# One PSUM tile and one exponential for four heads' scores, ScalarE statistics for one tile of the first norm, a q map with a minimum, and an attention sum on GpSimd

## The chip, the core and the metric

The kernel runs on one core of a Trainium2 chip. A core has a matrix engine (TensorE, PE in the profile, with its weight loads shown apart as PEld), a vector engine (VectorE, DVE), a scalar engine for functions of one argument (ScalarE, ACT), a general engine (GpSimd, POOL), and an engine that here only issues DMAs (SyncE, SP). Each engine works through its own list of instructions in order and waits on semaphores for the others. PSUM is the memory that matmuls write; SBUF holds everything else. The metric is device time in microseconds (us) of one execution; the median of several runs counts.

## What is computed

The input is x, 2048 tokens by 512, in bf16. A layer A (attention) and a layer B (a gated feed-forward network) follow one another twice, with the same weights in both rounds:

```python
x = x + A(layernorm(x)); x = x + B(layernorm(x))     # twice

# A: H = 32 heads of 16, N = 4 segments of L = 512 tokens
phi = lambda t: where(t > 0, t + 1, exp(t))
for s in range(N):
    logits = einsum('bhqd,bhkd->bhqk', qs, ks) * scale + mask      # causal
    a_dot = softmax(logits) @ vs
    a_mem = (phi(qs) @ M) / (phi(qs) @ z + 1e-6)
    outs.append(g * a_mem + (1 - g) * a_dot)                       # g = sigmoid(beta), one per head
    M = M + phi(ks)^T @ vs;  z = z + sum(phi(ks))
A = concat(outs) @ wo

# B: F = 1792
B = (gelu(x @ w_gate) * (x @ w_up)) @ w_down
```

## The kernel before

**Stages.** Two rounds of four segments are eight stages, k = 0 to 7, of 512 tokens each. Each stage has its norm, its products for q, k and v, its scores and their use, the output product wo, and its feed-forward part (gate, up, down). Large products are written as four matmuls on column tiles of 32 (`product`, L514 to L519).

**Who sets the order.** The instructions of all engines are put in order when the program is built, by a planner written in the kernel itself. It keeps a clock for each engine (`Clocks`), adds a fixed cost for each piece of work, and knows when each result should be there. Work for TensorE lies in `items`, sorted by due times (tables `DUE` and `BIAS`); an item is opened when its inputs are ready and one of the M_BANKS = 4 PSUM banks of kind m is free. Work for the other engines is posted with `post`, with a slack by which it may stand back. What comes out is a fixed list for each engine; on the chip only semaphores hold it together. When nothing is ready while scores remain, the planner inserts a warm product, which computes nothing that is used.

**Scores.** Each stage has STEPS = 20 score steps; a step is for four heads. `score_now` decides whether the next step is due, and whether both halves of it (two heads each) or only one: both if both PSUM score tiles are free by the planner's clock, one alone if TensorE is idle or in the stages below HALF_STEPS = 2. The list `st_free` holds when each half's tile is free. `scores` (L950 to L1008) writes the score matmuls (L971) into the tiles st0 and st1, one for each half and each of two banks, then for each half one exponential on ScalarE from PSUM to SBUF (L1002, 128 x 1024, pt<-st in the profile) and the causal masks on GpSimd (L989). Both tiles have a single buffer:

```python
            sts = {n: psp.tile([P, 2, L], F32, tag=f"st{n}", bufs=1, name="st") for n in halves}
```

Scores of even heads read k from the tile kf, those of odd heads from its copy kB.

**Use of the scores.** `flush_item` (L1010 to L1117) multiplies the probabilities with the values (pt and vaug, L1036), whose extra column per head holds a constant so that the row sum comes with the product. Then DVE transposes (L1060), takes the reciprocal (L1064), scales into ab (L1068), transposes back into aT (L1075) and adds the memory's part, aT + amT (L1079). A flush is ready when all masks of its steps are done by the planner's clock.

**Around them.** The class Norm (L529 to L628) takes the statistics of four token tiles (`stats` L543, `aggr` L552), on POOL their variance plus epsilon (L560) and its power -0.5 (rs, L566), and writes the normed rows xn (L580): on DVE, but on POOL in stage k = 5, which XNP = 32 says. `phi_q` (L755 to L773) makes phi of q from an exponential (L761), a clamp (L764) and an add with two inputs (L768). `upd` and `mem` (L802 to L926) carry M and z; mblk (L899) is a 32 x 128 piece on POOL. The very first norm (L1269 to L1320) is written out by hand, since nothing runs beside it: `first_stats` (L1276) and `first_aggr` (L1279) on DVE for four tiles, `first_scale` (L1282 and L1284) on POOL for two tiles at a time. `gate` (L459) prepares sigmoid(beta) on DVE, and L456 copies the constant column into three value tiles (vaugs) on ScalarE.

## Time and profile before

| | |
|---|---|
| runs | 549.41, 549.94, 551.12 us |
| median | 549.94 us |
| profiled execution | 549.15 us |
| its span | 547.2 us |
| mean granted TensorE clock | 1.0 |
| masks on POOL (L989) | 416, of 128 x 256 (336), 128 x 512 (72) and 128 x 1024 (8) |
| attention adds on DVE (L1079) | 28: 20 of 128 x 512, mean 541 ns, and 8 of 128 x 256, mean 281 ns |
| xn on POOL (L580) | 4, mean 2088 ns |
| DMA traffic | 28.90 MB in all, mean 53 GB/s |

The profile is of one execution, taken on the chip. The span runs from the first to the last instruction; the execution's own time has 2 us more. The profiled execution lies 0.8 us below the median, so a sum that starts from its rows starts from 549.15 and has to be moved by 0.8 us to be compared with medians. A line "L1002" is line 1002 of the kernel before; "pt<-st" are the names of what is written and read. In a group's row, "x320 | 309.6, 1029 | 53.7 <-PE st L971 47.9" says 320 instructions, 309.6 us busy, 1029 ns each on average, 53.7 us idle just before them, of which 47.9 ended with a score matmul. In a timeline, the two numbers in front are the start and the length in us of a run of like instructions, which overlap in TensorE's pipeline, so the distance between starts is what a step costs there.

### The profile page before, as it was taken

Reading aid. Unit: us, or ns where it says so; the run is one execution under the profiler, and the core shown is the slowest. Engines: PE = TensorE matmul, PEld = TensorE weight load, DVE = VectorE, ACT = ScalarE, POOL = GpSimd, SP = SyncE. Lnnn points to the kernel's source line nnn. Section 1 sums busy time; section 2 is a strip of 40 time slices with the busy share of each in tenths; the row PEclk is TensorE's granted clock in tenths of the full one; section 3 lists DMA queues with packets and bytes.
Section 4 is the critical chain, followed back from the end, with each engine's and each line's share of the span. In section 5 each row is a group of like instructions: output and inputs, shape, how many; then the busy total and the mean of one; then the engine's idle time right before and its main releaser. Section 6 shows DMA issues by size and latency. Waiting matters only on the chain.

```text
span 547.2 us, 25413 instructions
## 1 busy us (share of the span) xinstructions
PE 541.5 (99%) x11388; PEld 267.9 (49%) x11388; DVE 431.4 (79%) x814; ACT 443.3 (81%) x533; POOL 259.3 (47%) x516
## 2 busy tenths in 40 slices
PE   8999999999999999999999999999999999999997
PEld 4333345344454444444444444444445445445997
DVE  5988996899869989679776898589876999777162
ACT  5999999998999778977799879997889777882600
POOL 4786674556624678147551465056643472121000
PEclk9999999999999999999999999999999999999999
DMA  7357710622123025301140123111530113102101
GB/s 232 49 151 192 139 37 6 158 30 50 32 50 62 3 41 80 51 13 22 22 70 2 23 41 60 32 17 27 80 60 4 22 22 75 27 2 52 32 5 41
DMA packets 69756, 28.90 MB, mean 53 GB/s; under 512 B 59216, under 2 KB 69200, under 8 KB 69648
## 3 DMA queue, kind: packets, MB, share of 16 engines
q1 hardware_dynamic: 69504, 27.28, 25.0%
q8 instruction: 89, 1.46, 1.2%
q14 instruction: 19, 0.16, 0.1%
q10 hardware_dynamic: 144, 0.01, 0.0%
HBM read 9.71 MB, written 2.10 MB: 22 GB/s over the span
## 4 chain that ended last, share of the span: by engine, by line
PE 95%; POOL 2%; DVE 1%; DMA 1%; ACT 1%; issue 0%; POOLq 0%
PE m L519 76%; PE st L971 11%; PE m L1036 7%; POOL xn L580 2%; PE m L884 1%; DMA x_sb<-in_A_x_dram 1%; ACT pt L1002 1%; DVE st L1276 0%; POOL pt L989 0%; PE m L623 0%; DVE st L543 0%; PE m L936 0%; DVE x_sb L1134 0%; PE m L931 0%; POOL rs L566 0%
## 5 line engine op out<-in xcount | busy, mean ns | idle before, releaser
L1002 ACT ACTIVATE pt<-st 128x1024 bf16<-128x1024 f32 x320 | 309.6, 1029 | 53.7 <-PE st L971 47.9
L989 POOL TENSOR_SCALAR_AFFINE_SELECT pt<-pt 128x512 bf16<-128x512 bf16 (+2 forms) x416 | 204.5, 510 | 221.4 <-ACT pt L1002 213.7
L519 PE MATMUL m<-xnT,wu_sb 128*32 128x512 bf16 (+1 forms) x2016 | 106.6, 356 | 0.0
L519 PE MATMUL m<-xnT,wg_sb 128*32 128x512 bf16 (+1 forms) x2016 | 106.4, 356 | 0.0
L519 PE MATMUL m<-wd_sb,gel 128*32 128x512 bf16 (+2 forms) x1848 | 106.5, 373 | 0.0
L1223 DVE TENSOR_TENSOR gel<-gel,m 128x512 bf16<-128x512 bf16 x112 | 75.2, 683 | 36.0 <-PE m L519 30.0
L519 PEld LDWEIGHTS <-wu_sb 128*32 128x32 bf16 x2016 | 51.6, 97 | 40.0 <-issue 6.1
L519 PEld LDWEIGHTS <-wg_sb 128*32 128x32 bf16 x2016 | 51.6, 97 | 38.1 <-issue 4.4
L519 PEld LDWEIGHTS <-gel 128*32 128x32 bf16 x1848 | 50.8, 97 | 39.5 <-issue 5.0
L1060 DVE STREAM_TRANSPOSE byq<-m 128x512 f32<-128x512 f32 x64 | 45.4, 710 | 21.4 <-PE m L1036 21.0
L1134 DVE TENSOR_TENSOR x_sb<-x_sb,m 128x512 bf16<-128x512 bf16 (+1 forms) x65 | 42.2, 665 | 14.8 <-PE m L519 14.7
L1036 PE MATMUL m<-pt,vaug 128*32 128x256 bf16 (+3 forms) x1088 | 46.9, 293 | 0.5 <-POOL pt L989 0.4
L971 PE MATMUL st<-q,kB 32*128 32x256 bf16 (+3 forms) x544 | 40.9, 291 | 0.0
L543 DVE BATCH_NORM_STATS2 st<-x_sb 128x6 f32<-128x512 bf16 x60 | 40.5, 676 | 0.4
L971 PE MATMUL st<-q,kf 16*128 16x256 bf16 (+3 forms) x544 | 39.8, 294 | 0.1
L1036 PEld LDWEIGHTS <-vaug 128*32 128x32 bf16 x1088 | 25.2, 97 | 22.1 <-issue 5.9
L519 PE MATMUL m<-xnT,wq_sb 128*32 128x512 bf16 x496 | 34.2, 381 | 0.0
L519 PE MATMUL m<-xnT,wk_sb 128*32 128x512 bf16 x496 | 33.9, 380 | 0.0
L1188 ACT ACTIVATE gel<-m 128x512 bf16<-128x512 f32 x56 | 30.7, 602 | 3.6 <-PE m L519 3.4
L519 PE MATMUL m<-wv_sb,xnT 128*32 128x512 bf16 x512 | 33.5, 380 | 0.0
L971 PEld LDWEIGHTS <-kf 16*128 16x128 bf16 x544 | 12.4, 91 | 43.0 <-issue 41.7
L519 PE MATMUL m<-wo_sb,aT 128*32 128x512 bf16 x512 | 31.6, 380 | 0.0
(95 smaller groups left out, 550.7 us busy)
## 6 DMA issues: line engine op xcount, KB each, us to landing
out_dram<-x_sb SPq DMA_DIRECT2D x15, 128.0 KB, 1.8
wg_sb<-in_B_w_gate_dram SPq DMA_DIRECT2D x8, 224.0 KB, 3.6
kB<-kf SPq DMA_DIRECT2D x28, 64.0 KB, 2.9
wu_sb<-in_B_w_up_dram SPq DMA_DIRECT2D x8, 224.0 KB, 3.8
wd_sb<-in_B_w_down_dram SPq DMA_DIRECT2D x7, 256.0 KB, 3.9
x_sb<-in_A_x_dram SPq DMA_DIRECT2D x3, 512.0 KB, 6.5
xnT<-xn SPq DMA_TRANSPOSE x56, 2.5
x_sb<-in_A_x_dram SPq DMA_DIRECT2D x4, 128.0 KB, 3.0
```

What stands on the lines that cost most here:

```text
L519: nc.tensor.matmul(out[r], lhsT=lhsT[:, r], rhs=rhs, start=start, stop=stop, tile_position=(0, 32 * c))
L543: nc.vector.bn_stats(out=self.st6[:, 0, :], in_=x_sb[:, self.tt0 + j, :])
L580: eng.tensor_scalar(out=xn[:], in0=x_sb[:, self.tt0 + j, :], scalar1=self.mv[:, j, 0:1], scalar2=self.rs[:, j, :], op0=ALU.subtract, op1=A ...
L884: nc.tensor.matmul(psm()[r, b, :], lhsT=self.phik[:, j, b * P + 32 * c:b * P + 32 * c + 32], rhs=by_head(self.vaug)[:, j, h:h + 2, 0:DH], ...
L971: nc.tensor.matmul(sts[j // 2][:, j % 2, c0:c0 + q1 - q0], lhsT=lhsT[rows, b, P * ki:P * ki + P], rhs=self.q[rows, b, q0:q1], start=True, ...
L989: nc.gpsimd.affine_select(out=dv, in_=dv, pattern=[[0, w], [1, P]], compare_op=ALU.is_ge, fill=0.0, base=0, channel_multiplier=-1)
L1002: 1.024, lambda st=st, tile2=tile2: nc.scalar.activation(out=tile2[:], in_=st[:], func=ACT.Exp, scale=SCALE), told), table="exp")
L1036: nc.tensor.matmul(ps()[32 * j:32 * j + 32, q0 + shift:q1 + shift], lhsT=self.vaug[:, ki, h * (DH + 1):h * (DH + 1) + 32], rhs=step["pt"][ ...
L1060: nc.vector.transpose(out=self.byq[:, c], in_=ps()[:])
L1134: ck.dve.post(ck.made(), slack, (0.15 + 0.533 * n / D, lambda: nc.vector.tensor_tensor(out=xt, in0=xt, in1=ps()[:, 0:n], op=ALU.add), lamb ...
L1188: return lambda: nc.scalar.activation(out=out(), in_=in_(), func=ACT.Gelu_apprx_tanh)
L1223: ck.dve.post(ck.made(), NORMAL, (0.683, lambda: nc.vector.tensor_tensor(out=hidden(g, h), in0=hidden(g, h), in1=banked(ps), op=ALU.mult), ...
```

## The change

In words, in the order of the diff:

- The two score tiles become one, st, of 128 x 4 x 512 in PSUM (four banks, one buffer), and so do the two tiles for probabilities.
- From k = 1 on (JOIN = 1) a step that is scored whole has one exponential, 128 x 2048, instead of two of 128 x 1024, and its masks cover four heads instead of two. Where a step is scored in halves, there are still two exponentials, on two parts of the tiles. In k = 0 there are always two.
- In the first norm ScalarE takes the sum and the sum of squares of the fourth tile with two accumulating activations, and DVE scales them; the constant column of two value tiles goes to POOL, and the gate's two small operations are posted for later.
- phi of q becomes min(exp(q), max(q, 0) + 1): one operation with two scalars and one with two inputs, instead of a clamp and a three-way add.
- aT + amT is written for GpSimd instead of VectorE.
- xn is always on VectorE.
- The planner's constants and tables (N3, FLUSH_WAIT, LAST_FIRST, SHIFT, HALVED, DUE, BIAS and others) have other values, so the order on all engines is another. The tables are left out below.

```diff
 M_BANKS = 4
+JOIN = 1
...
-N3 = 0.0
+N3 = 44.0
...
-FLUSH_WAIT = 5.228
+FLUSH_WAIT = -0.017
...
-XNP = 32
...
-LAST_FIRST = 8
+LAST_FIRST = 2
...
+HALVED = {NK - 1}
+SHIFT = 0.8
...
+    st = psp.tile([P, 4, L], F32, tag="st", bufs=1, name="st")
...
-        nc.scalar.activation(out=by_head(va)[:, :, :, DH], in_=cden[:].unsqueeze(1).to_broadcast([P, TPS, H]),
-                             func=ACT.Copy)
+    def sums_column(i):
+        return by_head(vaugs[i])[:, :, :, DH], cden[:].unsqueeze(1).to_broadcast([P, TPS, H])
...
+        ck.dve.post(14.0, NORMAL, (0.6, gate, None))
...
-            if self.on_pool:
-                ck.pool.post(ready, self.slack, (1.62, xn, told))
-            else:
-                ck.dve.post(ready, self.slack, (0.5, xn, told))
+            ck.dve.post(ready, self.slack, (0.5, xn, told))
...
-            def clamp():
-                nc.vector.tensor_scalar(out=self.phiq[:, two, :], in0=self.phiq[:, two, :], scalar1=1.0, scalar2=None,
-                                        op0=ALU.min)
-
-            def add():
-                nc.vector.scalar_tensor_tensor(out=self.phiq[:, two, :], in0=self.q[:, two, :], scalar=0.0,
-                                               in1=self.phiq[:, two, :], op0=ALU.max, op1=ALU.add)
+            def linear():
+                self.lin = wrk.tile([P, 2, L], BF16, tag="lin", bufs=1, name="lin")
+                nc.vector.tensor_scalar(out=self.lin[:], in0=self.q[:, two, :], scalar1=0.0, scalar2=1.0,
+                                        op0=ALU.max, op1=ALU.add)
+
+            def least():
+                nc.vector.tensor_tensor(out=self.phiq[:, two, :], in0=self.phiq[:, two, :], in1=self.lin[:], op=ALU.min)
 
             ck.act.post(max(ready, ck.pe), slack, (1.06, exp, lambda t: ck.dve.post(
-                t, PHI_SLACK, (0.47, clamp, None),
-                (1.29, add, lambda t2: ev.update({("phiq", self.k, b): t2 for b in (2 * half, 2 * half + 1)})))), table="exp")
+                t, PHI_SLACK, (0.47, linear, None),
+                (0.75, least, lambda t2: ev.update({("phiq", self.k, b): t2 for b in (2 * half, 2 * half + 1)})))), table="exp")
...
-                pt = [wrk.tile([P, 2, L], BF16, tag="pt", bufs=2 * PT_STEPS, name="pt") for _ in range(2)]
+                pt = wrk.tile([P, 4, L], BF16, tag="pt", bufs=PT_STEPS, name="pt")
...
-            sts = {n: psp.tile([P, 2, L], F32, tag=f"st{n}", bufs=1, name="st") for n in halves}
...
-                    nc.tensor.matmul(sts[j // 2][:, j % 2, c0:c0 + q1 - q0], lhsT=lhsT[rows, b, P * ki:P * ki + P],
+                    nc.tensor.matmul(st[:, j, c0:c0 + q1 - q0], lhsT=lhsT[rows, b, P * ki:P * ki + P],
...
-            for n in halves:
-                st, tile2 = sts[n], pt[n]
-                blocks = tile2[:].rearrange("p j (a c) -> p j a c", c=P)
-                flat = tile2[:].rearrange("p j (a c) -> p (j a) c", c=P)
-                where = {(0, 1, 2, 3): [(flat, 8)], (0, 2): [(flat[:, 0:8:2, :], 4)]}.get(
-                    diag, [(blocks[:, :, a, :], 2) for a in diag])
+            joined = halves == (0, 1) and k >= JOIN
+            for n0, n1 in [(0, 2)] if joined else [(n, n + 1) for n in halves]:
+                heads, w = slice(2 * n0, 2 * n1), 2 * (n1 - n0)
+                blocks = pt[:, heads, :].rearrange("p j (a c) -> p j a c", c=P)
+                flat = pt[:, heads, :].rearrange("p j (a c) -> p (j a) c", c=P)
+                where = {(0, 1, 2, 3): [(flat, 4 * w)], (0, 2): [(flat[:, 0:4 * w:2, :], 2 * w)]}.get(
+                    diag, [(blocks[:, :, a, :], w) for a in diag])
                 done = []
-                step["masked"].append(done)
-                st_free[n] = 1e9
+                step["masked"].append((n1 - n0, done))
+                st_free[n0:n1] = [1e9] * (n1 - n0)
 
                 def mask(dv, w):
                     nc.gpsimd.affine_select(out=dv, in_=dv, pattern=[[0, w], [1, P]], compare_op=ALU.is_ge,
                                             fill=0.0, base=0, channel_multiplier=-1)
 
-                def told(a, n=n, where=where, done=done):
-                    st_free[n] = a
+                def told(a, n0=n0, n1=n1, where=where, done=done):
+                    st_free[n0:n1] = [a] * (n1 - n0)
                     if not where:
                         done.append(a)
                         return
...
                                               for m, (dv, w) in enumerate(where)])
 
                 ck.act.post(max(begun + 0.4, step["at"]), EXP_SLACK, (
-                    1.024, lambda st=st, tile2=tile2: nc.scalar.activation(
-                        out=tile2[:], in_=st[:], func=ACT.Exp, scale=SCALE), told), table="exp")
+                    0.17 + 0.427 * w, lambda heads=heads: nc.scalar.activation(
+                        out=pt[:, heads, :], in_=st[:, heads, :], func=ACT.Exp, scale=SCALE), told), table="exp")
...
-                    nc.vector.tensor_tensor(out=self.aT[:, b, where], in0=self.aT[:, b, where],
+                    nc.gpsimd.tensor_tensor(out=self.aT[:, b, where], in0=self.aT[:, b, where],
...
-                        ck.when(lambda: ("amT", k, b) in ev, lambda: ck.dve.post(
-                            max(t, ck.pe), soon, (0.18 + 0.0167 * nq, add, there)))
+                        ck.when(lambda: ("amT", k, b) in ev, lambda: ck.pool.post(
+                            max(t, ck.pe), soon, (0.2 + 0.08 * nq, add, there)))
...
+    sums = wrk.tile([P, 1, 2], F32, tag="sums", bufs=1, name="sums")
+    junk = wrk.tile([P, L], BF16, tag="e0", bufs=1, name="junk")
+    nc.scalar.activation(out=junk[:], in_=x_sb[:, TPS - 1, :], func=ACT.Copy, scale=-1.0 / D, accum_out=sums[:, :, 0])
+    nc.scalar.activation(out=junk[:], in_=x_sb[:, TPS - 1, :], func=ACT.Square, bias=sums[:, 0, 0:1], accum_out=sums[:, :, 1])
+    nc.scalar.activation(out=sums_column(0)[0], in_=sums_column(0)[1], func=ACT.Copy)
...
-    first_stats(3)
-    first_aggr(3)
+    nc.vector.tensor_tensor(out=n0.mv[:, TPS - 1:TPS, :], in0=sums[:], in1=parts[:], op=ALU.mult)
...
-    a0.made()
-    n0.first_rows = [n0.normed(j, j) for j in range(2)]
-    gate()
-    n0.first_rows += [n0.normed(j, j) for j in range(2, TPS)]
+    a0.made[0](), a0.made[1]()
+    n0.first_rows = [n0.normed(j, j) for j in range(TPS)]
```

## The prediction

> **What bounds the kernel now.** I read the page's busy shares first, then its chain, then the timelines of TensorE (PE) and ScalarE (ACT) in the first segment, where the change rearranges most.

> ```profile
> PE 541.5 (99%) x11388; PEld 267.9 (49%) x11388; DVE 431.4 (79%) x814; ACT 443.3 (81%) x533; POOL 259.3 (47%) x516
> ...
> PE 95%; POOL 2%; DVE 1%; DMA 1%; ACT 1%; issue 0%; POOLq 0%
> ...
> L1002 ACT ACTIVATE pt<-st 128x1024 bf16<-128x1024 f32 x320 | 309.6, 1029 | 53.7 <-PE st L971 47.9
> ```

> TensorE is busy for 541.5 of 547.2 us and carries 95% of the chain; the other three engines have at least a fifth of the span to spare. Removing work from ACT, DVE or Pool therefore earns nothing by itself. What counts is TensorE's own instructions, and any gap put between them. The next windows (start:end, length, then busy us of PE, PEld, DVE, ACT and POOL, clock, DMA share, GB/s) show how little gap there is now:

> ```profile
> 12.00:110.00 98.00, 97.90 (x1856) 40.91 (x1856) 84.03 (x163) 95.38 (x117) 61.94 (x127) 1.00 0.48 106
> 110.00:300.00 190.00, 189.51 (x3896) 87.63 (x3892) 157.39 (x298) 166.89 (x201) 102.60 (x202) 1.00 0.22 38
> ```

> In the first 98 us TensorE lacks 0.1 us, at full clock, and ACT is almost as full (95.4 of 98). That is where an exponential and the score after it can least afford to wait for each other. Today they do not: the two halves of a step (two heads each) have PSUM tiles of their own, so PE scores one half while ACT reads the other.

> ```profile
> 30.55 9.60 ACT L1002 ACTIVATE pt<-st 128x1024 bf16<-128x1024 f32 x10
> ...
> 34.05 0.39 PE L971 MATMUL st<-q,kf 16*128 16x512 bf16 x2
> 34.37 0.40 PE L519 MATMUL m<-xnT,wk_sb 128*32 128x512 bf16 x4
> 34.70 0.39 PE L971 MATMUL st<-q,kf 16*128 16x512 bf16 x2
> 35.02 0.62 PE L519 MATMUL m<-xnT,wk_sb 128*32 128x512 bf16 x8
> 35.46 0.39 PE L519 MATMUL m<-xnT,wq_sb 128*32 128x512 bf16 x4
> 35.78 0.39 PE L971 MATMUL st<-q,kf 16*128 16x384 bf16 x4
> 36.10 0.73 PE L1036 MATMUL m<-pt,vaug 128*32 128x512 bf16 x16
> 36.77 0.39 PE L971 MATMUL st<-q,kf 16*128 16x384 bf16 x4
> ```

> Ten exponentials run back to back at 0.96 us each. From score to score TensorE needs 0.65 us with one product between (34.05 to 34.70), 1.08 with three (34.70 to 35.78), so 0.86 with two, and 0.99 with a flush (35.78 to 36.77). Nothing waits.

> **Part 1: one PSUM tile for four heads.** This is the term that decides. The new tile st serves all steps, also those whose halves are still scored apart: 9 steps of k=0 and 10 of k=1 in the order that the changed program, built, issues. There the first matmul of a step's second half carries a semaphore count that is reached only by the exponential of the *same* step's first half, though that reads the other two heads; and the first half waits for the previous step's second exponential. Before, each half waited for its own half of the step before. So a pair that overlapped becomes a round: score, exponential, score. Its length comes from these rows:

> ```profile
> 11.67 0.40 PE L971 MATMUL st<-q,kf 16*128 16x512 bf16 x4
> ...
> 12.10 1.94 ACT L1002 ACTIVATE pt<-st 128x1024 bf16<-128x1024 f32 x2 [1.89 <-PE st L971]
> ...
> 43.34 2.85 ACT L1002 ACTIVATE pt<-st 128x1024 bf16<-128x1024 f32 x3 [0.52 <-POOL pt L989]
> ...
> 44.41 0.39 PE L971 MATMUL st<-q,kf 16*128 16x512 bf16 x2
> ```

> From a score's start to its exponential's start 0.43 us (11.67 to 12.10); the exponential 1.02 (1029 ns on the page; 43.34 to 44.36 for the first of three here); from its end to the score that it frees 0.05 (44.36 to 44.41). Together 1.50 us for each half. TensorE takes its instructions in order, so whatever is queued behind the waiting score (products, flushes) waits too; the products that lie between two scores cover only their own 0.65 to 1.08 us. In the built order 38 such edges lie in or behind split steps: 17 with two products, 6 with a flush, 6 with three products, one each at 0.65, 0.77 and 1.04 (mixtures, by the same rows), 6 long enough to wait for nothing. The stall is 17 x 0.64 + 6 x 0.51 + 6 x 0.42 + 0.85 + 0.73 + 0.46 = 18.5 us. Five more edges lead from a step scored whole to a split one, where 0.05 + 0.43 + 1.94 = 2.42 is needed and 1.49, 1.71, 1.82, 2.04 and 2.36 are there: 2.7. In the one long row of single exponentials (k=1) two evictions by ACT of some 0.6 us stand between: about 0.7 of them is seen. Together **+21.9**; if a half takes 1.40 to 1.60 us, 18 to 26.

> From k=1 on, the steps scored whole have one exponential of 128x2048. It isn't in the trace; between 1.88 (1029 ns and twice the 427 by which it exceeds ScalarE's gelu of half its width, 602 ns at L1188) and 2.06 (twice 1029) I take 1.9, by the 1.94 of a pair in a row. It removes 130 instructions and some 20 us of ACT work, all beside TensorE: nothing. The first half's probabilities come later by 0.9 us, which I count under part 3.

> **Part 2: the order on TensorE.** 19 steps are split instead of 23. A half takes PE as long as a whole (0.32 us to the next instruction at 34.05, and 0.32 at 35.78), and the product between two scores takes 0.33 where 0.22 is its usual distance (two in 0.44 at 35.02): 0.42 for each split, -1.7. Two more warm products at 0.22: +0.4. Everything else on TensorE has the same count and shape.

> **Part 3: off TensorE.** The four xn that GpSimd (POOL) computed in one norm go to DVE. They took 8.30 us, masks stood behind them, and TensorE's starts fall 0.94 us behind there, of which its row names 0.42:

> ```profile
> 203.13 8.30 POOL L580 TENSOR_SCALAR xn<-x_sb,mv,rs 128x512 bf16<-128x512 bf16 x4
> 211.40 2.71 POOL L989 TENSOR_SCALAR_AFFINE_SELECT pt<-pt 128x256 bf16<-128x256 bf16 x6
> 211.86 0.64 PE L1036 MATMUL m<-pt,vaug 128*32 128x384 bf16 x6 [0.42 <-POOL pt L989]
> ```

> That goes: -0.9. The 28 attention adds go from DVE (0.54 us each) to POOL. POOL's nearest row with the same shape is xn at 2.09; by the growth of its masks with width (0.456, 0.697, 1.116 us for 256, 512 and 1024 columns) it would be lower, so I take 1.4, between 0.54 and 2.09: 39 us against 37 saved on masks (416 become 250: 72 x 0.456 + 144 x 0.697 + 30 x 1.116 + 4 x 2.0 = 175 instead of 212) and 8 on xn. POOL stays at half busy. What it can cost: a mask queued behind an add, and so a flush. From score to last mask takes about 3.1 us now with 2.3 to spare before the flush; with the joined exponential it is 3.4, and the built order puts most flushes 3.4 to 4.2 us behind their score. That cover is thin: +0.8, from 0 to 5. The q map as a minimum saves DVE some 7 us of its 1.30 us adds, beside TensorE: nothing. At the start ACT takes the fourth tile's statistics off DVE, but the reciprocal root behind it stays on POOL: -0.2 (-0.6 to +0.2).

> **Sum**: 21.9 - 1.7 + 0.4 - 0.9 - 0.2 + 0.8 = +20.3 us. The profiled execution took 549.15 us (span 547.2), so 569.5 on its scale; the median of the runs, 549.94, lies 0.8 above it, so **570.2 us**. A difference of about 0.3% (1.65 us) is what a measurement of this kernel can tell from none.

> **Rivals.** *Not slower* (0.05): the score's wait ends before it binds, because a half's round is no longer than the work between two scores. It decides at 0.86 us a round, the commonest distance. Then only the small terms are left, -1.6: 548.3, on the border of faster and same. For it: no exponential holds up a score anywhere in the trace of before. Against it: the 1.02 us exponential alone, wholly inside the round, is already longer than 0.86.

> *The clock falls* (0.08): with a wait after every half, TensorE is busy in little over half of these stretches. At the start of before, where it had just begun, its warm products stood 0.427 us apart until about 5 us, and 0.21 after. At that pace the work between the scores of the 32 stalled edges, 17 x 0.86 + 6 x 0.99 + 6 x 1.08 + 2.5 = 29.5 us, would take 59 instead of 29.5 + 18.5: +11, so 581. Against it: no wait here is longer than 1 us, and by the page the clock stays at full from its second slice to the end.
> [...]

> *POOL's adds hold up flushes* (0.07): from k=2 on slack is 0.1 to 0.7 us, and an add ahead of a flush's last mask delays it by up to 1.4. If 8 of the 28 do so by 1 us, +8: 578. For it: masks of 256 columns beside DVE's scaling of ab took 0.77 us on average where 0.41 is their median, so POOL and DVE hold each other up. Against it: POOL is idle half of the time.
> [...]

> **How the numbers follow.** Serial halves as summed: 0.80, own range 562 to 578 (a round of 1.40 to 1.60, flush waits of 0 to 5). The range has to hold 8 in 10: nine tenths of that case (0.72), the POOL case (0.07) and part of the clock case, so 561 to 581. Faster 0.03 and same 0.03 are the not-slower case with a little for a smaller stall; slower is the rest, 0.94.

> **What would show it.** In the changed kernel's profile: waits of "PE st" for "ACT pt" of about 0.5 to 0.65 us each, some 30 of them, all before k=2; single exponentials about 1.5 us apart from start to start in k=1; TensorE some 20 us short of full in the first 130 us, at clock 1.0; the joined exponential near 1.9 us; no xn on POOL. Later windows as full as before. If TensorE is gap-free in the first 130 us, the prediction is wrong at its main step; if it is full there and short later, POOL's adds are the cause; if the clock is under 1.0, the second rival.

## The result, and the profile after

The changed kernel took 576.53 us (median; 575.11 to 577.78), the kernel before 550.36 us beside it: ratio 1.0475, interval 1.0446 to 1.0504, or 26.2 us slower. The forecast was 570.2 us in a range of 561 to 581. The profiled execution took 576.83 us, its span 575.0.

First the page of the changed kernel: busy times, the granted TensorE clock in 40 slices, the chain that ended last, and the group of the exponentials.

```profile
PE 558.2 (97%) x11396; PEld 268.1 (47%) x11396; DVE 419.5 (73%) x793; ACT 438.0 (76%) x402; POOL 239.2 (42%) x378
...
PEclk9979965799999999999999999999999999999999
...
PE 89%; ACT 8%; issue 1%; DMA 1%; SPq 0%; DVE 0%; ACTq 0%
...
L1029 ACT ACTIVATE pt<-st 128x2048 bf16<-128x2048 f32 (+1 forms) x190 | 304.4, 1609 | 84.2 <-PE st L997 66.3
```

ScalarE has come onto the chain with 8%, and the clock row, all nines before, has a hole in its third slice (29 to 43 us) and a longer one from the sixth to the eighth (72 to 115 us). TensorE is busy 16.7 us longer with eight matmuls more, which is the mark of a slower clock, and idle 11.1 us longer (16.8 of its span instead of 5.7): together the 27.8 us of the span. The same two windows as before show where:

```profile
12.00:110.00 98.00, 86.18 (x1204) 31.41 (x1199) 61.52 (x126) 70.18 (x80) 49.70 (x106) 0.79 0.35 79
110.00:300.00 190.00, 189.71 (x4040) 89.47 (x4036) 154.78 (x294) 165.13 (x143) 91.72 (x129) 1.00 0.27 46
```

In the first 98 us TensorE lacks 11.8 us, its clock is 0.79 on average, and it gets through 1204 instructions instead of 1856. After 110 us it is as full as it was. The list of TensorE's waits, empty of scores before, is headed by this (us in total, times, longest):

```profile
PE st L997 <- ACT pt L1029: 10.9, 22, 0.9
```

The chain in order of time shows the round itself (start, length, what), first at full clock, then at half clock:

```profile
32.83 0.41 PE st L997 x4
33.24 0.02 issue
33.26 1.03 ACT pt L1029
34.29 0.04 issue
34.33 0.40 PE st L997 x2
...
82.48 0.62 PE st L997 x4
83.10 0.02 issue
83.12 1.03 ACT pt L1029
84.15 0.04 issue
84.19 0.62 PE st L997 x2
```

Score, exponential, score, with nothing in parallel: 1.50 us from 32.83 to 34.33, as worked out in the prediction, and 1.71 from 82.48 to 84.19, where the score takes 0.62 instead of 0.41.

### The profile page after: what moved, and what is told of

It is laid out like the page before. It is cut to its first block, busy times and chain, and to the rows that moved or that the text cites. A ratio compares the mean times of both kernels' runs of the same rounds, so it can differ in the third digit from the quotient of the medians.

```text
span 575.0 us, 25060 instructions
## 1 busy us (share of the span) xinstructions
PE 558.2 (97%) x11396; PEld 268.1 (47%) x11396; DVE 419.5 (73%) x793; ACT 438.0 (76%) x402; POOL 239.2 (42%) x378
## 4 chain that ended last, share of the span: by engine, by line
PE 89%; ACT 8%; issue 1%; DMA 1%; SPq 0%; DVE 0%; ACTq 0%
PE m L542 70%; PE st L997 11%; ACT pt L1029 7%; PE m L1063 6%; DMA x_sb<-in_A_x_dram 1%; PE m L911 0%; SPq L389 0%; PE m L641 0%; ACT kf L534 0%; PE m L963 0%; PE m L958 0%; ACT junk L1317 0%; ACT junk L1316 0%; ACT vaug L534 0%; ACT e L811 0%
## 5 line engine op out<-in xcount | busy, mean ns | idle before, releaser
L1029 ACT ACTIVATE pt<-st 128x2048 bf16<-128x2048 f32 (+1 forms) x190 | 304.4, 1609 | 84.2 <-PE st L997 66.3
L1016 POOL TENSOR_SCALAR_AFFINE_SELECT pt<-pt 128x512 bf16<-128x512 bf16 (+3 forms) x250 | 166.1, 678 | 248.2 <-ACT pt L1029 247.1
L542 PEld LDWEIGHTS <-gel 128*32 128x32 bf16 x1848 | 46.2, 97 | 44.6 <-issue 4.2
L1063 PE MATMUL m<-pt,vaug 128*32 128x256 bf16 (+3 forms) x1088 | 48.5, 303 | 0.0
L997 PEld LDWEIGHTS <-kf 16*128 16x128 bf16 x544 | 14.1, 92 | 53.2 <-issue 52.4
L1063 PEld LDWEIGHTS <-vaug 128*32 128x32 bf16 x1088 | 27.3, 99 | 22.8 <-issue 5.2
L542 PE MATMUL m<-xnT,wq_sb 128*32 128x512 bf16 x496 | 36.3, 396 | 0.0
L542 PE MATMUL m<-wo_sb,aT 128*32 128x512 bf16 x512 | 36.3, 410 | 0.0
L1106 POOL TENSOR_TENSOR aT<-aT,amT 128x512 bf16<-128x512 bf16 (+1 forms) x28 | 28.3, 1018 | 19.1 <-DVE aT L1102 14.9
L542 PE MATMUL m<-xnT,wk_sb 128*32 128x512 bf16 x496 | 36.1, 400 | 0.0
```

The lines of the kernel that those rows point to most:

```text
L542: nc.tensor.matmul(out[r], lhsT=lhsT[:, r], rhs=rhs, start=start, stop=stop, tile_position=(0, 32 * c))
L997: nc.tensor.matmul(st[:, j, c0:c0 + q1 - q0], lhsT=lhsT[rows, b, P * ki:P * ki + P], rhs=self.q[rows, b, q0:q1], start=True, stop=True, ti ...
L1016: nc.gpsimd.affine_select(out=dv, in_=dv, pattern=[[0, w], [1, P]], compare_op=ALU.is_ge, fill=0.0, base=0, channel_multiplier=-1)
L1029: 0.17 + 0.427 * w, lambda heads=heads: nc.scalar.activation(out=pt[:, heads, :], in_=st[:, heads, :], func=ACT.Exp, scale=SCALE), told), ...
L1063: nc.tensor.matmul(ps()[32 * j:32 * j + 32, q0 + shift:q1 + shift], lhsT=self.vaug[:, ki, h * (DH + 1):h * (DH + 1) + 32], rhs=step["pt"][ ...
L1106: nc.gpsimd.tensor_tensor(out=self.aT[:, b, where], in0=self.aT[:, b, where], in1=self.amT[b][:, where], op=ALU.add)
```

## The experiments

All times are medians, with the kernel before in the same series.

**Two tiles again.** The changed kernel, with the PSUM tile split; nothing else in the order of TensorE, VectorE and SyncE differs.

```diff
-    st = psp.tile([P, 4, L], F32, tag="st", bufs=1, name="st")
+    sts = [psp.tile([P, 2, L], F32, tag=f"st{n}", bufs=1, name="st") for n in range(2)]
...
-                    nc.tensor.matmul(st[:, j, c0:c0 + q1 - q0], ...
+                    nc.tensor.matmul(sts[j // 2][:, j % 2, c0:c0 + q1 - q0], ...
...
-                        out=pt[:, heads, :], in_=st[:, heads, :], func=ACT.Exp, scale=SCALE), told)
+                        out=pt[:, 2 * n:2 * n + 2, :], in_=sts[n][:], func=ACT.Exp, scale=SCALE)
+                        for n in range(n0, n1)], told)
```

> The changed kernel with the score tile split again into two PSUM tiles of two heads each; every joined exponential becomes two of 128x1024 (about 20 us more ScalarE work), all else and the order on TensorE, VectorE and SyncE unchanged. Theory (the one tile makes a half wait for the other half's exponential): the waits of scores for exponentials go, the clock stays at 1.0, and what is left are the small terms, 548.5 us (547 to 550.5). Rival (the new order, the adds on GpSimd or the longer latency cost most of it): 560 us or more, with TensorE short of full after 110 us too.

Measured: 549.14 us against 550.45, ratio 0.9976 (0.9955 to 0.9998), clock 1.0. Its two windows:

```profile
12.00:110.00 98.00, 97.30 (x1856) 40.92 (x1852) 83.36 (x164) 94.82 (x118) 59.92 (x118) 1.00 0.43 102
110.00:300.00 190.00, 189.95 (x3916) 88.34 (x3908) 156.97 (x297) 168.29 (x202) 90.16 (x127) 1.00 0.24 40
```

The 11.8 us that TensorE lacked are 0.7, and no score waits for an exponential. The rival, that the order or the adds on POOL cost most of it, falls: the whole loss (26.2 us, and the 1.3 that come free) hangs on the shared tile. This run also takes the joined exponential apart; the one called Mixed, below, keeps it from k = 2 on and is as fast, so there the joining is not the cause.

**One tile in the kernel before.** The other direction: only this part of the change.

```diff
+    st4 = psp.tile([P, 4, L], F32, tag="st", bufs=1, name="st")
...
-            sts = {n: psp.tile([P, 2, L], F32, tag=f"st{n}", bufs=1, name="st") for n in halves}
...
-                st, tile2 = sts[n], pt[n]
+                st, tile2 = st4[:, 2 * n:2 * n + 2, :], pt[n]
```

> The kernel before with one change, the two score tiles made one tile of four heads; two exponentials as before, order unchanged. Theory: the same serial rounds, in 23 split steps instead of 19 and with some whole steps following within 2.4 us, so about 25 to 30 us of waits, and some 6 us more where the clock falls: 580 us (570 to 590), clock below 1.0 in the first 110 us. Rival (the tile alone is harmless, the loss comes from the order that was made with it): 553 us or less.

Measured: 584.16 us, ratio 1.061 (1.0567 to 1.0652), or 33.7 us slower; clock of the profiled run 0.968. First its list of waits, then ScalarE's timeline where the kernel before had ten exponentials in 9.60 us:

```profile
PE st L972 <- ACT pt L1003: 17.9, 36, 1.2
...
29.88 1.02 ACT L1003 ACTIVATE pt<-st 128x1024 bf16<-128x1024 f32 x1 [0.78 <-PE st L972]
31.65 1.02 ACT L1003 ACTIVATE pt<-st 128x1024 bf16<-128x1024 f32 x1 [0.75 <-PE st L972]
33.43 1.02 ACT L1003 ACTIVATE pt<-st 128x1024 bf16<-128x1024 f32 x1 [0.76 <-PE st L972]
```

They start 1.77 us apart there, at half clock (0.73 on average from 30 to 45 us). The tile alone does it, and does more than in the changed kernel, whose order has fewer split steps: of its 17.9 us of waits 6.6 come after 110 us, where the changed kernel has 0.2, and its clock falls four times instead of three (0.968 on average over the span, against 0.964). How much of the difference each of these makes is not shown.

**Filling the waits.** To part the clock from the waits, the changed kernel computes during them: up to two products after each split half are issued twice.

```diff
+        if fills[0]:
+            fills[0] -= 1
+            product_once(out, lhsT, rhs, start, False)
+            start = False
+        product_once(out, lhsT, rhs, start, stop)
...
         att[k].scores(t, halves)
+        fills[0] = 2 if k < 2 and halves != (0, 1) else 0
```

> The changed kernel with up to two products after each score half of k=0 and k=1 issued twice, 65 in all, 14 us of TensorE work at full clock, so that it computes while it would wait; those products count twice in their sums. Theory (the clock is granted by how full TensorE is, and its fall costs about 6 us on top of the waits): the clock stays at 1.0 and the time falls though work was added, to about 570.5 us (568 to 573). Rival (the fall has another cause, or costs nothing because the waits only get shorter): clock near 0.96 again and 576 us or more.

Measured: 571.98 us, ratio 1.0394 (1.0354 to 1.0434): 21.5 us over the kernel before instead of 26.2, though TensorE does 14 us more (65 products; four matmuls take 0.216 us in the changed kernel at full clock, the median distance of their starts). From its page:

```profile
PE 555.8 (98%) x11656; PEld 277.3 (49%) x11656; DVE 419.3 (74%) x793; ACT 438.4 (77%) x402; POOL 239.3 (42%) x378
...
PEclk9999999999999999999999999999999999999999
```

The clock stays full, 1.0 on average. So the waits by themselves are worth at most 571.98 less 549.14, 22.8 us (an added product that finds no wait would add its own time), and the clock's fall at least 4.6 on top (the two intervals leave about 2.7 either way). The rounds say that the added products cost next to nothing: ahead of the first fall, six single exponentials in a row take 7.67 us from the first start to the last in both kernels (25.59 to 33.26 in the changed one, 26.07 to 33.74 here). And they give the same price for the clock: the three longest rows of single exponentials last, from first start to last, 14.55, 4.79 and 29.83 us in the changed kernel and 13.77, 4.59 and 26.03 here, 4.8 us less.

**No split steps.**

```diff
-        return (0,) if free[0] and (idle and k >= HALF_FROM or k < HALF_STEPS and not other) else ()
+        return ()
```

> The changed kernel without split steps: every step is scored whole, and the order is made anew, so it allows for the wait. Theory: a whole step frees the tile 2.42 us after its start (k=0) or 2.36 (joined), which the order knows and fills with products; ScalarE is nearly full in the first 98 us, so a part is lost there: 555 us (550 to 562), clock 1.0, few waits of scores for exponentials. Rival (the loss is ScalarE's rate behind one buffer, not the order's ignorance): 570 us or more.

Measured: 566.72 us, ratio 1.0291 (1.0253 to 1.033). This missed its range of 550 to 562, and lies below the 570 of its rival. The order allows for the wait, but finds too little to put there. First the warm products' group in this kernel, then in the changed kernel, then this kernel's windows:

```profile
L542 PE MATMUL m<-warm 128*32 128x512 bf16 x308 | 23.2, 409 | 1.0 <-DVE am L866 0.5
```

```profile
L542 PE MATMUL m<-warm 128*32 128x512 bf16 x56 | 4.3, 384 | 0.0
```

```profile
12.00:110.00 98.00, 94.64 (x1952) 43.84 (x1952) 79.55 (x160) 89.51 (x105) 52.79 (x97) 1.00 0.48 113
110.00:300.00 190.00, 185.34 (x3748) 84.01 (x3744) 151.09 (x277) 152.71 (x117) 90.38 (x129) 0.98 0.18 32
```

There are 77 warm products instead of 14 (four matmuls each), the 63 more some 13.6 us of computing for nothing at 0.216 each, and TensorE lacks 3.4 and 4.7 us in the two windows: 2.5 us are four scores that wait for an exponential, the rest are other waits. The clock falls here too, once, for the 6.8 us behind a stretch from 148.52 to 151.93 us in which TensorE was busy for 1.39 of 3.41 us. ScalarE does less than before in the same time (89.5 of 98 us instead of 95.4). That with one buffer it stands still during each score is an estimate, from the 0.48 us that single exponentials of the changed kernel waited for theirs at full clock (33.26, 34.76); that this, and not the planner's skill, sets the 566.7 us is not shown.

**Mixed.** Two tiles while steps are split (k below 2), one tile and the joined exponential after.

```diff
+            if k == 2 and t == 0:
+                one_tile()        # closes the pool of the two tiles and opens one of 128 x 4 x 512
...
-                    nc.tensor.matmul(sts[j // 2][:, j % 2, c0:c0 + q1 - q0], ...
+                    nc.tensor.matmul((whole[0][:, j] if whole else sts[j // 2][:, j % 2])[:, c0:c0 + q1 - q0], ...
```

> The changed kernel with two score tiles in k=0 and k=1, where steps are split, and the one tile with joined exponentials (128x2048) from k=2 on, where every step is whole; k=1's whole steps have two exponentials; order on TensorE, VectorE and SyncE as in the changed kernel. Theory (only split steps pay for the one tile, and the joined exponential is off the path): the same as with two tiles throughout, 549 us (547.5 to 550.5), clock 1.0, ScalarE some 17 us less busy than there. Rival (joined exponentials bring their masks, and so the flushes, too late): 551 us or more, with waits of pt matmuls for masks after k=2.

Measured: 548.62 us against 549.87, ratio 0.9973 (0.9949 to 0.9997), clock 1.0: the same as two tiles throughout, within the intervals. The masks are in time: the only wait of a pt matmul for one in its list is of 0.3 us, in k = 0. But ScalarE is only 7 us less busy (434.8 instead of 442.0), not 17. Its two forms:

```profile
L1041 ACT ACTIVATE pt<-st 128x2048 bf16<-128x2048 f32 x120 | 225.4, 1878 | 56.1 <-PE st L1009 41.6 <-POOL pt L1028 13.0 <-POOL mblk L934 0.9
L1043 ACT ACTIVATE pt<-st 128x1024 bf16<-128x1024 f32 x80 | 76.3, 1031 | 4.7 <-PE st L1009 4.5
```

A joined exponential takes 1.88 us; two in a row took 1.94, since their ends overlap (80 take 76.3, not 82.5). Joining saves 0.06 us a step, 7 in all.

**The sums on VectorE.** Two tiles throughout, with the other engine for aT + amT.

```diff
-                    nc.gpsimd.tensor_tensor(out=self.aT[:, b, where], in0=self.aT[:, b, where],
+                    nc.vector.tensor_tensor(out=self.aT[:, b, where], in0=self.aT[:, b, where],
```

> The kernel with two tiles throughout, and the 28 attention sums written for VectorE again at the places where the order has them for GpSimd. Theory (the sums are off the path on either engine): within 1 us of the kernel with two tiles, 549 us (548 to 550.5). Rival (on GpSimd they block VectorE's two-input operations and cost several us): 546 us or less.

Measured: 549.59 us against 549.87, ratio 0.9988 (0.9969 to 1.0007). With the sums on GpSimd it was 0.9976 and 0.9973. Either engine will do; the rival falls.

**Fullness and clock.** A kernel of its own, whose stages hold TensorE at different shares of its time. A line of STAGES reads products per round, exponentials per round, rounds.

```python
STAGES = [(None, 0, 120), (4, 1, 27), (None, 0, 60), (3, 1, 27), (None, 0, 60), (2, 1, 27), (None, 0, 60), (1, 1, 27),
          (None, 0, 60), (6, 2, 17), (None, 0, 60), (4, 2, 17), (None, 0, 60)]
```

> A kernel that computes none of the reference: it copies x to the output, and beside that TensorE runs stages of about 40 us. In four of them a round is a score (two matmuls), one exponential of 128x1024 that reads it, and 4, 3, 2 or 1 products of the kernel's form, so that TensorE computes for about 1.3, 1.1, 0.86 or 0.65 of 1.50 us; in two, two exponentials and 6 or 4 products, about 1.7 or 1.3 of 2.46 us. Between them it runs 60 products without a pause. Theory (the clock goes by how full TensorE is over some us, and pauses of 0.2 to 0.85 us are enough): 1.0 with 4 products, under 1.0 after a few us with 2 and 1, 3 products in between and open; of the two longer rounds 4 products falls too. Rival (only an idle stretch of some us closes the gate): 1.0 in every stage.

This is one execution. At full clock rounds came out at 1.56 us and, with two exponentials, at 2.62. The first fence has the windows of the stages with 4 and 3 products, then, in steps of 5 us, the beginning of the stage with 2, and a score there with the wait ahead of it; the second the stage with 6 products and two exponentials, a score there, and the beginning of the last stage, with 4.

```profile
32.00:70.00 38.00, 33.33 (x444) 12.48 (x436) 0.00 (x0) 25.06 (x25) 0.00 (x0) 1.00 0.00 1
87.00:125.00 38.00, 27.86 (x344) 9.86 (x337) 0.00 (x0) 24.77 (x25) 0.00 (x0) 1.00 0.01 2
...
140.00:145.00 5.00, 3.12 (x38) 0.90 (x30) 0.00 (x0) 3.38 (x4) 0.00 (x0) 1.00 0.00 0
145.00:150.00 5.00, 3.98 (x30) 0.99 (x30) 0.00 (x0) 2.80 (x4) 0.00 (x0) 0.58 0.02 3
...
141.03 0.39 PE L59 MATMUL st<-wide,w 16*128 16x512 bf16 x2 [0.63 <-ACT pt L67]
```

```profile
267.00:300.00 33.00, 22.36 (x326) 9.02 (x326) 0.00 (x0) 25.61 (x26) 0.00 (x0) 1.00 0.00 1
...
273.26 0.39 PE L59 MATMUL st<-wide,w 16*128 16x512 bf16 x2 [0.82 <-ACT pt L67]
...
320.00:325.00 5.00, 2.50 (x40) 0.91 (x32) 0.00 (x0) 3.92 (x4) 0.00 (x0) 1.00 0.00 0
325.00:330.00 5.00, 3.38 (x34) 0.97 (x31) 0.00 (x0) 4.09 (x4) 0.00 (x0) 0.67 0.00 0
```

Busy for 88% (33.33 of 38) and 73% (27.86 of 38), the clock stays at 1.0. At 62% (3.12 of 5) it is half within 10 us, and with one product too (0.50 from 212 to 245 us). In the longer rounds 68% (22.36 of 33) stays at 1.0 and 50% (2.50 of 5) falls, to 0.67 in the next 5 us. In these stages the share decides, not the length of one pause: at 68% TensorE stood still for 0.82 us of each 2.62 us round and kept its clock, at 62% for 0.63 of each 1.56 and lost it. The rival, that only an idle stretch of some us lowers the clock, falls.

Over what time the share counts, the records of the granted clock say. In every trace here the clock's changes lie a whole number of stretches of 3.41 us apart; in the changed kernel it is half from 35.84 to 42.67, from 56.32 to 59.73 and from 76.80 to 107.52 us, for two, one and nine of them. All eleven falls inside the kernels (three in the changed kernel, behind 55%, 65% and 61%; one without split steps, behind the 1.39 of 3.41 us above; three here, the first behind 58%; four with one tile in the kernel before) come at the end of a stretch in which TensorE was busy for 40 to 65%. Two stretches of this kernel, each with the one behind it:

```profile
142.43:145.84 3.41, 1.99 (x22) 0.69 (x21) 0.00 (x0) 2.16 (x3) 0.00 (x0) 1.00 0.00 0
145.84:149.25 3.41, 3.01 (x22) 0.61 (x20) 0.00 (x0) 2.05 (x2) 0.00 (x0) 0.50 0.02 5
...
296.03:299.44 3.41, 1.81 (x28) 0.74 (x27) 0.00 (x0) 2.77 (x3) 0.00 (x0) 1.00 0.00 0
299.44:302.85 3.41, 2.59 (x40) 1.07 (x43) 0.00 (x0) 2.37 (x3) 0.00 (x0) 1.00 0.00 0
```

No exact limit comes out of this: behind 58% (1.99 of 3.41) the clock fell, behind 53% it did not. The profile only models the ends of matmuls, so its shares are rough. But no stretch above 65% was followed by a fall in these traces, and after a fall the clock came back only behind stretches of 94 to 100% (3.41 of 3.41 us each time in the changed kernel).

## Why the prediction was right, and where it was not

**The mechanism** was the one named: a half that waits for the other half of the same step. Undoing the tile takes the loss away, making the tile alone brings it, and the round on the chip is the 1.50 us that three rows of before gave.

**The main term** was +21.9 us; with the clock held, it measures at most 22.8.

**The clock** was treated as a rival with a chance of 0.08, +11 us and all of the stalled work slowed down. It came, in part of the stretch and cheaper. The step that failed is the argument against it, that no wait is longer than 1 us: that the length of a wait counts was not shown by the trace of before. In these runs it did not matter; the share of busy time in a stretch of 3.41 us did. Ahead of its three falls the changed kernel was busy for 55% (1.88 of 3.41 us), 65% and 61%, with no score waiting longer than 0.9 us:

```profile
29.01:32.43 3.42, 2.30 (x36) 0.83 (x29) 2.80 (x6) 2.40 (x3) 1.83 (x6) 1.00 0.23 82
32.43:35.84 3.41, 1.88 (x23) 0.63 (x24) 0.52 (x1) 2.39 (x3) 3.41 (x4) 1.00 0.02 5
35.84:39.25 3.41, 3.27 (x26) 0.75 (x25) 2.38 (x6) 1.99 (x2) 2.17 (x5) 0.50 0.25 57
...
52.91:56.32 3.41, 2.23 (x28) 0.89 (x24) 3.34 (x8) 2.10 (x3) 1.32 (x3) 1.00 0.86 277
56.32:59.73 3.41, 3.41 (x40) 1.25 (x40) 2.64 (x7) 2.52 (x3) 1.30 (x5) 0.50 1.09 159
...
73.39:76.80 3.41, 2.07 (x24) 0.67 (x24) 0.30 (x1) 2.39 (x3) 1.75 (x5) 1.00 1.29 138
76.80:80.21 3.41, 3.05 (x36) 0.96 (x32) 1.12 (x3) 1.93 (x3) 1.17 (x3) 0.50 1.08 321
```

The price was mis-sized as well. Some 20 rounds ran at half clock, not the 32 that the prediction doubled. Between 77 and 104 us the rounds with two products took 1.71 to 1.79 us from score to score, about the 1.72 that doubling gives, but those with a flush 1.73 to 1.81 instead of 1.98, and those with three products 1.94 instead of 2.16. The whole came to 4.6 us, not 11. With it the sum of 20.3 would have been some 25, against 26.2 measured; the rest is 0.9 in the main term and 0.3 in the small ones. The last sign of the prediction, a clock under 1.0 for the rival in place of the main step, was too sharp: both came together, and the time stayed inside the range because the clock cost less than half of its price.

**The checks** named some 30 waits of 0.5 to 0.65 us and 20 us of idling. The profile has 22 waits and 11.8 us, because at half clock the products fill what would have been a pause (3.05 to 3.41 of 3.41 us in the windows above). The single exponentials of k = 1 were to start 1.5 us apart; most stand 1.7 to 2.0 apart, at half clock.

**The small terms** came to -1.6 us in the sum; both kernels without the false wait show -1.3, with intervals from about -0.1 to -2.8, which can't part them one by one. The wait behind POOL's xn is gone (after 110 us TensorE lacks 0.05 of 190 us with two tiles, 0.49 before). The +0.8 for thin flushes was too much; with two tiles one such wait of 0.3 us is left. The joined exponential (1.9 assumed, 1.88 measured) saves ScalarE about 7 us, not the 20 of the prediction, which set it against two lone exponentials though the row of a pair, 1.94, was in its own fence. GpSimd's sum was taken at 1.4 us; its two forms in the changed kernel:

```profile
L1106 POOL TENSOR_TENSOR aT<-aT,amT 128x512 bf16<-128x512 bf16 x20 | 23.1, 1157 | 9.1 <-DVE aT L1102 5.2 <-DMA amT<-am 3.8
L1106 POOL TENSOR_TENSOR aT<-aT,amT 128x256 bf16<-128x256 bf16 x8 | 5.2, 670 | 9.9 <-DVE aT L1102 9.7 <-DMA amT<-am 0.2
```

That is twice VectorE's 541 ns, and by the run with the sums on VectorE without an effect on the time that these runs could see.

## What to carry to other kernels

When two buffers are merged so that one instruction can read both, look at what still uses them one at a time: here the wait is kept for the tile, not for the part that is read, and 19 split steps out of 160 paid for it. An order written by a planner is only as good as the waits it knows; check in the built program which instruction's count a wait really names. And before joining instructions on an engine with time to spare, ask what the joining can earn: here 0.06 us of ScalarE a step, off the path.
